# Attention and a gated feed-forward layer: byte-wise dependencies in the list scheduler, and v's and the weights' statistics taken several at a time

## The chip, the core and the metric

The kernel runs on one core of one Trainium2 chip. The metric is the device time of one execution in microseconds. Six names stand for the core's parts below: PE (TensorE, matmuls), PEld (the loading of a matmul's stationary operand), DVE (VectorE), ACT (ScalarE), POOL (GpSimd) and SP (SyncE, which issues transfers here). The engines run side by side, each strictly through its own list of instructions, and meet at semaphores.

## The reference

Eight batches, twelve heads, 448 positions, 64 channels per head. q and k are normalised (root mean square over the channels, times a gain), then attention:

```python
q_n, k_n = (rmsnorm(q, g_q), rmsnorm(k, g_k))
scores = scale * np.matmul(q_n, k_n.transpose(0, 1, 3, 2))
attn = np.exp(scores - np.max(scores, axis=-1, keepdims=True))
attn = attn / (np.sum(attn, axis=-1, keepdims=True) + 1e-09)
x = np.matmul(attn, v)                   # heads side by side: 768 channels
```

The result x goes, per batch, into a feed-forward layer that mixes each position with the one before it:

```python
xk = mu_k * x + (1.0 - mu_k) * x_prev
xr = mu_r * x + (1.0 - mu_r) * x_prev
k = np.maximum(xk @ w_k, 0.0)            # 768 -> 1024
v = k * k @ w_v                          # 1024 -> 768
r = 1.0 / (1.0 + np.exp(-(xr @ w_r)))    # 768 -> 768
out = r * v
```

The three weight matrices come in 64-bit numbers.

## The kernel before

**Numbers.** Most products are made from two float16 halves, a high part and the remainder: three matmuls (high by high, high by low, low by high) stand for one. To split a number well, it is first scaled by a power of two that is taken from a statistic of its tile.

**Attention.** Two heads are a *pair* (48 in all, six per batch), two pairs a *quad*. For each quad k and q are loaded, normalised and turned so that channels lie on partitions (tile `stk`). Seven groups of scores per quad follow (`sc`, five banks of PSUM): DVE finds the largest of each row, ACT takes the exponential and its sum (tile `sums`), DVE makes the reciprocals, and the probabilities are written, turned, to `pT`. Then a pair's product of `pT` with v (called av) is made into a PSUM bank called `ot`. There is one such bank. In batch 0 (quads 0 to 2, pairs 0 to 5, the constant `U32`) all this is done in float32; later pairs use the halves `vh` and `vl` of v.

**v's statistics** (`vprep`). For each pair ACT squares v and sums each partition's squares to one column, `vs`. PE spreads that column over all partitions, with a matmul against the identity into bank `ot`: the column is its stationary operand, read as the upper half of a float32, that is as bfloat16. DVE takes the maximum, makes a power of two `sv` from its exponent in two steps and the inverse `iv` in a third (in `bstat`, six columns of each per batch); then ACT writes `vh` and DVE `vl`. Two buffers `vf` take v as it is loaded, and in batch 0 av reads `vf` itself.

**The weights** (`weights`, `wsplit`). Twenty tiles (8 of w_k, 6 of w_r, 6 of w_v) are turned from 64-bit to float32 (`wf`), and each gets its scale: a matmul of the tile with itself, DVE takes the diagonal (`dg`), a matmul with ones spreads it, DVE takes the maximum and makes the scale in `WSC` and the inverse in `WIN`, one column per tile. Then the tile is split into `wkh`/`wkl`, `wrh`/`wrl` or `wvh`/`wvl`. For the first tiles the buffers `raw` and `wf` are partly borrowed from the later tile `kk`. The inverses are first used when the eight tiles of w_k are done (`RSC`) and when all twenty are (`wdone == NW`).

**The feed-forward layer** (`mixk`, `mixr`, `moe`). As soon as all six pairs of a batch are attended, xk is mixed, and PE makes the products with w_k (into bank `mm`, of which there are two), then with w_r and w_v. The products of batch b are interleaved with the attention of the next.

**What sets the order.** Nothing above is written in the order in which it runs. Each part is a generator that yields its operations, and the class `Plan` is a list scheduler: it keeps a clock for each engine and prices for the operations, and always emits the yielded operation whose start, less a bonus for its priority, is earliest. A start is the later of the engine's clock and the moment at which the operation's operands are free, plus a margin on PE (1200 ns for the matmul of vs). To know the latter, the scheduler records for each operation which tiles it reads and writes, each as a range of elements along the free dimension: `span` (line 142) makes the ranges, `ready` (line 226) compares them. What is emitted stands in the engine's list for good; the semaphores that keep the program right are set by the layer below, whatever the scheduler believes. All operations are recorded at one line, so the profile shows L265 for nearly everything (L272 in the changed kernel) and parts are told apart by tile names.

The lines around `vs`, for a later pair:

```python
yield A.activation(out=vh.bitcast(BF16), in_=vf, func=AF.Square, accum_out=vs[:, 0:1])
pt = yield from banks["ot"].get()
yield T.matmul(form=("v", 60), out=pt[:, 0:P], lhsT=vs[:, 0:1].bitcast(BF16)[:, 1:2]..., rhs=ident16, ...)
```

Of the kernel before, what the change touches and what calls it, by code (L numbers as in the profile page):

```python
# [10 lines left out]
I32 = mybir.dt.int32  # L11
AF = mybir.ActivationFunctionType
# [64 lines left out]
U32 = 3  # L77
SWITCH = 600
# [122 lines left out]
class Plan:  # L201
# [9 lines left out]
    def margin(self, form):  # L211
        if form == "moe":
            return 0
        if form == "av" and self.st["want"] != "xk":
            return MARGIN_A
        return MARGIN_V if form == "v" else MARGIN

# [196 lines left out]
def attn_moe_kernel(tc, q, k, v, g_q, g_k, mu_k, mu_r, w_k, w_v, w_r, out):  # L414
# [41 lines left out]
    LD, SS, VF, VV, TQ, PT, BS, BSC, XT, XK, XKN, XR, CNT, OS, CARRY = {}, {}, {}, {}, {}, {}, {}, {}, {}, {}, {}, {}, {}, {}, {}  # L456
# [6 lines left out]
    def until(f):  # L463
        while not f():
            yield f
# [56 lines left out]
    ring_sum = [small.tile([P, 6], F32, name="sums%d" % n, bufs=1) for n in range(6)]  # L522
# [129 lines left out]
    def turn(w, X, n, u):  # L652
        for a0 in range(0, NT, 4):
# [15 lines left out]
            if u < U32:  # L669
                dst = whole(X[:, n])[:, a0:a0 + m, :]  # L670
                if plan.clk["ACT"] < plan.clk["DVE"]:
# [27 lines left out]

    def vpreps():  # L700
        for i in range(NPAIR):
            st["vi"] = i
            yield from until(lambda: i in VF and st["tq"] >= GATE_V)
            if i < 2 * U32:
                yield from vprep(i, VF.pop(i), None, None)
                continue
            vh = yield from R["vh"].get()
            vl = yield from R["vl"].get()
            yield from vprep(i, VF.pop(i), vh, vl)

    def vprep(i, vf, vh, vl):
        b, hp = pairs[i]
# [3 lines left out]
        vs = small.tile([P, 2], F32, name="vs", bufs=4)  # L716
        if vh is None:
            pt = yield from banks["ot"].get()
            yield A.activation(out=pt.rearrange("p (a c) -> p a c", c=HD), in_=vf, func=AF.Square, accum_out=vs[:, 0:1])
        else:  # L720
            yield A.activation(out=vh.bitcast(BF16), in_=vf, func=AF.Square, accum_out=vs[:, 0:1])
            pt = yield from banks["ot"].get()
        yield T.matmul(form=("v", 60), out=pt[:, 0:P], lhsT=vs[:, 0:1].bitcast(BF16)[:, 1:2].broadcast_to([P, P]), rhs=ident16, start=True, stop=True)
        yield V.tensor_reduce(out=vs[:, 1:2], in_=pt[:, 0:P], axis=AX.X, op=ALU.max)
        banks["ot"].put(pt)
        sv, iv = s_[:, hp:hp + 1], s_[:, NP + hp:NP + hp + 1]
        yield V.tensor_scalar(out=sv.bitcast(I32), in0=vs[:, 1:2].bitcast(I32), scalar1=24, scalar2=23, op0=ALU.logical_shift_right, op1=ALU.logical_shift_left)
        yield V.tensor_scalar(out=sv.bitcast(I32), in0=sv.bitcast(I32), scalar1=-1.0, scalar2=float(204 << 23), op0=ALU.mult, op1=ALU.add)
        yield V.tensor_scalar(out=iv.bitcast(I32), in0=sv.bitcast(I32), scalar1=-1.0, scalar2=float(0x7F000000), op0=ALU.mult, op1=ALU.add)
        if vh is None:  # L730
            VV[i] = vf, None, None
        else:
# [4 lines left out]
        if hp == NP - 1:  # L737
            yield from batch_scales(b)
# [52 lines left out]
    def expo(gi, j, both, sums, D, tp):  # L791
        sp = both[j]
        if tp is not None:
            yield V.tensor_reduce(out=sums[:, j:j + 1], in_=sp[:, 0:S], axis=AX.X, op=ALU.max, negate=True)
            yield A.activation(out=tp.bitcast(F32).rearrange("p a c -> p (a c)")[:, j * S:(j + 1) * S], in_=sp[:, 0:S], func=AF.Exp, bias=sums[:, j:j + 1], accum_out=sums[:, 4 + j:5 + j])
# [7 lines left out]
    def probs(gi, both, sums, D, tp):  # L803
# [15 lines left out]
        r = sums[:, 2:4]  # L819
# [16 lines left out]
    def probs_pe(u, x, t0, sums, tp):  # L836
        r = sums[:, 2:4]
        yield V.tensor_scalar(out=r, in0=sums[:, 4:6], scalar1=1e-9, scalar2=2.0 ** -15, op0=ALU.add, op1=ALU.mult)
# [6 lines left out]
        for a0 in range(0, NT, 4):  # L845
# [6 lines left out]
            if u < U32:  # L852
                dst = whole(PTQ[:, :, :])[:, a0:a0 + m, c0:c0 + P]
                yield A.copy(out=dst, in_=src) if plan.clk["ACT"] < plan.clk["DVE"] else V.tensor_copy(out=dst, in_=src)
# [17 lines left out]
    def attends():  # L872
        for i in range(NPAIR):
# [17 lines left out]
            if vl is None:  # L891
                VFREE.append(vh)
# [92 lines left out]

    def wsplit(nm, kt, c, ci, f):
# [6 lines left out]
        sc, inv = WSC[:, ci:ci + 1], WIN[:, ci:ci + 1]  # L993
# [8 lines left out]
        yield V.tensor_scalar(out=inv.bitcast(I32), in0=sci, scalar1=-1.0, scalar2=float(0x7F000000), op0=ALU.mult, op1=ALU.add)  # L1002
# [164 lines left out]
```

## Time and profile before

| | us |
|---|---|
| median of 3 runs | 1048.58 |
| their range | 1046.12 to 1053.55 |
| the profiled execution | 1048.6 |
| its span, first to last instruction | 1046.8 |
| PE busy | 937.4 (90%) |
| DVE busy | 796.4 (76%) |
| ACT busy | 747.2 (71%) |
| POOL busy | 686.5 (66%) |

A row of a group gives the engine, the operation, output<-input by the program's names, the shapes and the number of instructions, then busy time in us and the mean of one in ns, then the idle time in front of them and what ended it. A row of a wait gives who waited for whom, with the sum in us, the number of times and the longest. A row in order of time gives start, length, engine and operation; in brackets the idle time in front of it and what ended that. PEclk, and the column of the same name in a table of stretches, is the clock that PE was granted as a share of full speed.

### The profile page before, as it was taken

The page shows a single profiled execution, that of the slowest core. Times are in us where ns is not written, and L with a number is a line of the kernel's source. Part 1 is how long each engine was busy: PE and PEld are TensorE (multiplying, and loading weights), DVE is VectorE, ACT ScalarE, POOL GpSimd, SP SyncE. Part 2 cuts the span into 40 slices and gives each one's busy share as a digit, 9 for nine tenths or more (in the row PEclk, how much of TensorE's full clock was granted, in tenths as well). Part 3 has the DMA queues.
Part 4 walks back from the last instruction along what each step waited for, and adds up shares of the span by engine and source line. Part 5 has one row for each costly group of instructions (what it writes and reads, how often), then busy time and mean ns, then how long its engine had stood idle before and what let it go on. Part 6 is the DMA issues. An engine that isn't in the chain of part 4 may idle for free. (4 is left out here: it accounts for less than half of the span.)

```text
span 1046.8 us, 18947 instructions
## 1 busy us (share of the span) xinstructions
PE 937.4 (90%) x6166; PEld 491.6 (47%) x6166; DVE 796.4 (76%) x2001; ACT 747.2 (71%) x1753; POOL 686.5 (66%) x738
## 2 busy tenths in 40 slices
PE   1678685788999999999999999999899999999997
PEld 0344332444554555455545555454345544555564
DVE  4888868997988688968987888879876887884100
ACT  2576748896879688788887778868786888874311
POOL 2587767862778565985796569857595569725811
PEclk9788876999999999999999999999799999999999
DMA  7443347884988799898986898688785897684011
GB/s 200 117 112 105 88 115 161 179 177 95 171 166 153 149 174 172 156 165 160 182 166 117 166 184 170 130 163 168 153 154 120 167 184 155 118 146 84 1 31 31
DMA packets 447043, 146.62 MB, mean 140 GB/s; under 512 B 418784, under 2 KB 443360, under 8 KB 446944
## 3 DMA queue, kind: packets, MB, share of 16 engines
q1 hardware_dynamic: 427408, 127.42, 64.1%
q10 hardware_dynamic: 19536, 18.00, 6.0%
q8 instruction: 48, 0.79, 0.3%
q14 instruction: 51, 0.42, 0.1%
HBM read 50.40 MB, written 11.01 MB: 59 GB/s over the span
## 5 line engine op out<-in xcount | busy, mean ns | idle before, releaser
L265 PE MATMUL mm<-wvh,kk 128*128 128x384 f16 x896 | 233.9, 326 | 0.0
L265 PE MATMUL mm<-xk,wkh 128*128 128x448 f16 x768 | 212.5, 359 | 7.5 <-DVE WSC L265 6.7
L265 DVE TENSOR_REDUCE sums<-sc 128x1 f32<-128x448 f32 x336 | 194.4, 615 | 31.8 <-PE sc L265 31.2
L265 ACT ACTIVATE sc<-sc,sums 128x448 f32<-128x448 f32 x294 | 181.3, 618 | 43.8 <-DVE sums L265 40.4
L265 PE MATMUL mm<-wrh,xr 128*128 128x384 f16 x672 | 178.2, 329 | 0.0
L265 ACT ACTIVATE nat<-sc,sums 128x448 f16<-128x448 f32 (+1 forms) x258 | 157.3, 650 | 26.4 <-DVE sums L265 18.8
L265 PEld LDWEIGHTS <-kk 128*128 128x128 f16 (+1 forms) x1362 | 129.8, 98 | 96.1 <-issue 12.9
L265 DVE SCALAR_TENSOR_TENSOR nat<-sc,sums,nat 128x448 f16<-128x448 f32 x228 | 148.7, 675 | 21.9 <-ACT nat L265 21.7
L265 PE MATMUL mm<-wvl,kk 128*128 128x384 f16 x448 | 146.0, 326 | 0.0
L265 PE MATMUL sc<-stk 64*128 64x448 f16 (+3 forms) x1104 | 132.8, 386 | 11.7 <-DVE nat L265 7.5
L265 PE MATMUL mm<-xk,wkl 128*128 128x448 f16 x384 | 137.4, 358 | 0.0
L265 PEld LDWEIGHTS <-xr 128*128 128x128 f16 x1008 | 96.2, 98 | 74.0 <-issue 14.3
L265 PEld LDWEIGHTS <-wkh 128*128 128x128 f16 x768 | 73.0, 99 | 82.9 <-issue 23.6
L265 PE MATMUL mm<-wrl,xr 128*128 128x384 f16 x336 | 110.3, 328 | 0.0
L265 PE MATMUL ot<-pT,vh 128*64 128x448 f16 x672 | 101.9, 360 | 4.8 <-DMA pT<-natx 2.0
L265 POOL TENSOR_TENSOR o<-o,bsc 128x384 f32<-128x384 f32 x48 | 42.7, 890 | 88.5 <-DVE o L265 55.7
L265 POOL TENSOR_TENSOR qk<-qk,ss 128x896 f32<-128x896 f32 x36 | 63.8, 1773 | 34.2 <-DVE ss L265 31.0
L265 ACT ACTIVATE o<-mm,bsc 128x128 f32<-128x128 f32 x144 | 45.3, 382 | 56.6 <-PE mm L265 44.2
L265 POOL TENSOR_TENSOR nat<-nat 128x448 f32<-128x448 f32 x46 | 54.0, 1175 | 39.0 <-ACT nat L265 38.7
L265 POOL TENSOR_TENSOR nat<-qk,nat 128x896 f16<-128x896 f32 x30 | 57.3, 1911 | 28.2 <-ACT nat L265 28.1
L265 DVE SCALAR_TENSOR_TENSOR o<-o,mm 128x384 f32<-128x384 f32 x56 | 30.6, 547 | 58.1 <-PE mm L265 57.9
L265 DVE SCALAR_TENSOR_TENSOR df<-x,bsc,df 128x448 f32<-128x448 f32 x68 | 64.8, 962 | 10.6 <-POOL df L265 10.5
(167 smaller groups left out, 1799.5 us busy)
## 6 DMA issues: line engine op xcount, KB each, us to landing
out_dram<-o SPq DMA_DIRECT2D x56, 192.0 KB, 3.1
qk<-in_k_dram SPq DMA_DIRECT2D x46, 224.0 KB, 3.8
qk<-in_q_dram SPq DMA_DIRECT2D x108, 64.0 KB, 2.6
vf<-in_v_dram SPq DMA_DIRECT2D x96, 64.0 KB, 2.7
raw<-in_moe_w_v_dram ACTq DMA_DIRECT2D x12, 512.0 KB, 4.8
vf<-in_v_dram SPq DMA_DIRECT2D x96, 48.0 KB, 2.4
raw<-in_moe_w_r_dram ACTq DMA_DIRECT2D x12, 384.0 KB, 3.3
kk<-in_moe_w_k_dram ACTq DMA_DIRECT2D x8, 384.0 KB, 3.9
```

Of the source, the lines that this page charges most:

```text
L265: r = op.fn(op.kw["out"], op.kw["value"]) if op.fn.__name__ == "memset" else op.fn(**op.kw)
```

## The change

Six edits:

- `span` gives ranges in bytes instead of elements (except for `pT`, whose ranges stay as they were). Two views of one tile with different element sizes are now compared rightly.
- In batch 0 `vprep` takes two pairs at a time: each is squared by itself, then two matmuls, one reduction over both, and each of the two steps on two columns. The inverses of the batch's six pairs are made in one step behind the last pair. The later pairs go one by one as before.
- In batch 0 a pair's v is handed to attention (`VV`) before its statistics; its buffer is given back when both the square and av are done (`vfree`).
- The inverses of the weights' scales are made for eight tiles at once, when w_k is done, and for the other twelve when all are.
- In `sums` the row sums and their reciprocals stand in every second column (4 and 6, 8 and 10) instead of side by side; the tile has 12 columns.
- `pick` replaces a comparison of two clocks by the same comparison.

```diff
@@ span
     if t.name.startswith("pT"):
         lo %= 2 * S
         hi = lo + x.ap[-1][1]
+    else:
+        lo, hi = lo * SIZE[x.dtype], hi * SIZE[x.dtype]
...
@@ vpreps, vprep
-        for i in range(NPAIR):
+        i = 0
+        while i < NPAIR:
             st["vi"] = i
...
+            n = V_SIDE if i < 2 * U32 else 1
+            yield from vprep([i + e for e in range(n)])
+            i += n
...
+        vs = small.tile([P, 4], F32, name="vs", bufs=4)
+        vh = vl = pt = None
+        for e, i in enumerate(js):
+            yield from until(lambda: i in VF and st["tq"] >= GATE_V)
+            vf = VF.pop(i)
+            if half:
+                vh = yield from R["vh"].get()
+                vl = yield from R["vl"].get()
+                sq = vh.bitcast(BF16)
+            else:
+                VV[i] = vf, None, None
+                pt = pt or (yield from banks["ot"].get())
+                sq = pt.rearrange("p (a c) -> p a c", c=HD)
+            yield A.activation(out=sq, in_=vf, func=AF.Square, accum_out=vs[:, e:e + 1])
+            if not half:
+                vfree(i, vf)
+                if e < n - 1:
+                    banks["ot"].put(pt)
+                    pt = None
+        pt = pt or (yield from banks["ot"].get())
+        yield [T.matmul(form=("v", 60 * n), out=pt[:, e * P:(e + 1) * P], lhsT=vs[:, e:e + 1].bitcast(BF16)[:, 1:2].broadcast_to([P, P]), rhs=ident16, start=True, stop=True) for e in range(n)]
+        yield V.tensor_reduce(out=vs[:, 2:2 + n], in_=pt[:, 0:n * P].rearrange("p (a c) -> p a c", c=P), axis=AX.X, op=ALU.max)
         banks["ot"].put(pt)
+        sv, iv = s_[:, hp:hp + n], s_[:, NP + hp:NP + hp + n]
...
-        yield V.tensor_scalar(out=iv.bitcast(I32), in0=sv.bitcast(I32), scalar1=-1.0, scalar2=float(0x7F000000), op0=ALU.mult, op1=ALU.add)
...
-        if hp == NP - 1:
+        if hp + n == NP:
+            if not half:
+                yield inverse(s_[:, NP:2 * NP], s_[:, 0:NP])
             yield from batch_scales(b)
...
@@ expo, probs, probs_pe
-    accum_out=sums[:, 4 + j:5 + j])
+    accum_out=sums[:, 4 + 2 * j:5 + 2 * j])
...
-        r = sums[:, 2:4]
+        r = sums[:, 8:11:2]
...
@@ wsplit
-        yield V.tensor_scalar(out=inv.bitcast(I32), in0=sci, scalar1=-1.0, scalar2=float(0x7F000000), op0=ALU.mult, op1=ALU.add)
...
         if ci < NF and st["wkeys"] == NF:
             yield from until(lambda: st["mus"])
+            yield inverse(WIN[:, 0:NF], WSC[:, 0:NF])
...
         if st["wdone"] == NW:
             yield from until(lambda: st.get("rsc"))
+            yield inverse(WIN[:, NF:NW], WSC[:, NF:NW])
```

Since the scheduler decides the order, the edits move instructions throughout. Three places follow; rows of the kernel before carry L265, rows of the changed one L272.

The first is PE's list at v's statistics of pair 10 (of 0 to 47), where the first products with w_r (`wrh`, `wrl`) begin. `stk` are the turned q and k, `xr` the mixed input. Before:

```order
L265 LDWEIGHTS stk_1874
L265 MATMUL sc_2482<-stk_1874 128x448
L265 LDWEIGHTS vs
L265 MATMUL ot_2526<-ident_75,vs 128x128
L265 LDWEIGHTS xr_1746
L265 MATMUL mm_2535<-wrh,xr_1746 128x384
```

and now:

```order
L272 LDWEIGHTS stk_2223
L272 MATMUL sc_2451<-stk_2223 128x448
L272 LDWEIGHTS vs
L272 MATMUL ot_2476<-ident_75,vs 128x128
L272 LDWEIGHTS stk_2223
L272 MATMUL sc_2481<-stk_2223 128x448
```

The matmul of vs stands at the same row of PE's list. Before, the first product follows it; now a group of scores stands between. By the numbers that the build gives to instructions in the order of their placing, the square of this pair on ACT was placed directly ahead of this matmul before (no other matmul between them), and 18 matmuls ahead of it now.

The second place is PE's list at pair 36, between the last products of one batch with w_v (`kk` by `wvh`, `wvl`) and the first of the next with w_k. Before:

```order
L265 LDWEIGHTS stk_8665
L265 MATMUL sc_9127<-stk_8665 128x448
L265 LDWEIGHTS vs
L265 MATMUL ot_9173<-ident_75,vs 128x128
L265 LDWEIGHTS stk_8665
L265 MATMUL sc_9167<-stk_8665 128x448
```

and now:

```order
L272 LDWEIGHTS kk_7838
L272 MATMUL mm_9086<-wvl,kk_7838 128x384
L272 LDWEIGHTS kk_7838
L272 MATMUL mm_9086<-wvh,kk_7838 128x384
L272 LDWEIGHTS vs
L272 MATMUL ot_9120<-ident_75,vs 128x128
```

Before, scores stand in front of the matmul of vs, with none placed between the square and it; now products with w_v do, and 12 of them were placed between.

The third place is DVE's list where the last weight tile is split (`wvl`). Before:

```order
L265 TENSOR_SCALAR WSC<-WSC 128x1
L265 TENSOR_SCALAR bstat<-vs 128x1
L265 TENSOR_SCALAR WIN<-WSC 128x1
L265 TENSOR_SCALAR bstat<-bstat 128x1
L265 SCALAR_TENSOR_TENSOR nat_2363<-sc_2295,sums_108,nat_2363 128x448
L265 TENSOR_SCALAR bstat<-bstat 128x1
L265 TENSOR_SCALAR sst<-sst 128x14
L265 TENSOR_SCALAR sst<-sst,gm 128x14
L265 TENSOR_REDUCE sums_109<-sc_2408 128x1
L265 SCALAR_TENSOR_TENSOR wvl<-wf_2231,WSC,wvh 128x8x128
```

and now:

```order
L272 TENSOR_REDUCE sums_110<-sc_2451 128x1
L272 SCALAR_TENSOR_TENSOR wvl<-wf_2291,WSC,wvh 128x8x128
L272 TENSOR_REDUCE sums_110<-sc_2452 128x1
L272 TENSOR_SCALAR WIN<-WSC 128x12
L272 SCALAR_TENSOR_TENSOR nat_2449<-sc_2366,sums_109,nat_2449 128x448
L272 TENSOR_SCALAR WIN<-WIN,smu 128x6
```

The inverse of one tile stood ahead of the split; now the inverses of twelve tiles stand behind it, ahead of the steps that use them. Up to this split DVE's list holds 28 instructions fewer than before (510 instead of 538), among them two reductions of scores more (71 instead of 69).

More of the change, by code (lines that the diff above doesn't have):

```diff
@@ L11 @@
 I32 = mybir.dt.int32
+SIZE = {F32: 4, I32: 4, F16: 2, BF16: 2, mybir.dt.uint8: 1}
 AF = mybir.ActivationFunctionType
@@ L77 @@
 U32 = 3
+V_SIDE = 2
 SWITCH = 600
@@ L216, in margin, with pick @@
         return MARGIN_V if form == "v" else MARGIN
+    def pick(self, a, b):
+        return a if self.clk[a] < self.clk[b] else b
     def now(self):
@@ L521, in attn_moe_kernel @@
             HOME[name, o] = vw
-    ring_sum = [small.tile([P, 6], F32, name="sums%d" % n, bufs=1) for n in range(6)]
+    ring_sum = [small.tile([P, 12], F32, name="sums%d" % n, bufs=1) for n in range(6)]
     def setup():
@@ L670, in turn @@
                 dst = whole(X[:, n])[:, a0:a0 + m, :]
-                if plan.clk["ACT"] < plan.clk["DVE"]:
+                if plan.pick("ACT", "DVE") == "ACT":
                     yield A.activation(out=dst, in_=src, func=AF.Copy, scale=gc[:, 0:1]) if n == 0 else A.copy(out=dst, in_=src)
@@ L698, in vload, with vfree, vprep @@
             VF[i] = vf
+    def vfree(i, vf):
+        FR[i] = FR.get(i, 0) + 1
+        if FR[i] == 2:
+            VFREE.append(vf)
     def vpreps():
-        for i in range(NPAIR):
+        i = 0
+        while i < NPAIR:
             st["vi"] = i
[L703 to L712, printed above, removed]
+            n = V_SIDE if i < 2 * U32 else 1
+            yield from vprep([i + e for e in range(n)])
+            i += n
+    def vprep(js):
+        b, hp = pairs[js[0]]
+        n, half = len(js), js[0] >= 2 * U32
         if hp == 0:
@@ L715, in vprep @@
         s_ = BS[b]
[L716 to L723, printed above, removed]
@@ L724, in vprep @@
-        yield V.tensor_reduce(out=vs[:, 1:2], in_=pt[:, 0:P], axis=AX.X, op=ALU.max)
+        vs = small.tile([P, 4], F32, name="vs", bufs=4)
[17 more added lines that the diff above has]
+                    pt = None
@@ L728, in vprep @@
+        yield V.tensor_scalar(out=sv.bitcast(I32), in0=vs[:, 2:2 + n].bitcast(I32), scalar1=24, scalar2=23, op0=ALU.logical_shift_right, op1=ALU.logical_shift_left)
         yield V.tensor_scalar(out=sv.bitcast(I32), in0=sv.bitcast(I32), scalar1=-1.0, scalar2=float(204 << 23), op0=ALU.mult, op1=ALU.add)
-        yield V.tensor_scalar(out=iv.bitcast(I32), in0=sv.bitcast(I32), scalar1=-1.0, scalar2=float(0x7F000000), op0=ALU.mult, op1=ALU.add)
-        if vh is None:
-            VV[i] = vf, None, None
-        else:
+        if half:
+            yield inverse(iv, sv)
@@ L794, in expo @@
             yield V.tensor_reduce(out=sums[:, j:j + 1], in_=sp[:, 0:S], axis=AX.X, op=ALU.max, negate=True)
-            yield A.activation(out=tp.bitcast(F32).rearrange("p a c -> p (a c)")[:, j * S:(j + 1) * S], in_=sp[:, 0:S], func=AF.Exp, bias=sums[:, j:j + 1], accum_out=sums[:, 4 + j:5 + j])
+            yield A.activation(out=tp.bitcast(F32).rearrange("p a c -> p (a c)")[:, j * S:(j + 1) * S], in_=sp[:, 0:S], func=AF.Exp, bias=sums[:, j:j + 1], accum_out=sums[:, 4 + 2 * j:5 + 2 * j])
             banks["sc"].put(sp)
@@ L836, in probs_pe @@
     def probs_pe(u, x, t0, sums, tp):
-        r = sums[:, 2:4]
-        yield V.tensor_scalar(out=r, in0=sums[:, 4:6], scalar1=1e-9, scalar2=2.0 ** -15, op0=ALU.add, op1=ALU.mult)
+        r = sums[:, 8:11:2]
+        yield V.tensor_scalar(out=r, in0=sums[:, 4:7:2], scalar1=1e-9, scalar2=2.0 ** -15, op0=ALU.add, op1=ALU.mult)
         yield V.reciprocal(out=r, in_=r)
@@ L853, in probs_pe @@
                 dst = whole(PTQ[:, :, :])[:, a0:a0 + m, c0:c0 + P]
-                yield A.copy(out=dst, in_=src) if plan.clk["ACT"] < plan.clk["DVE"] else V.tensor_copy(out=dst, in_=src)
+                yield A.copy(out=dst, in_=src) if plan.pick("ACT", "DVE") == "ACT" else V.tensor_copy(out=dst, in_=src)
             else:
@@ L891, in attends @@
             if vl is None:
-                VFREE.append(vh)
+                vfree(i, vh)
             else:
@@ L984, in weights, with inverse @@
             plan.spawn(wsplit(nm, kt, c, ci, f), wprio)
+    def inverse(o, i):
+        return V.tensor_scalar(out=o.bitcast(I32), in0=i.bitcast(I32), scalar1=-1.0, scalar2=float(0x7F000000), op0=ALU.mult, op1=ALU.add)
     def wsplit(nm, kt, c, ci, f):
@@ L992, in wsplit @@
         yield [T.matmul(form=("w", 110 * kt), out=pg[:, 0:P], lhsT=w16[:, i, :], rhs=w16[:, i, :], start=(i == 0), stop=(i == kt - 1)) for i in range(kt)]
-        sc, inv = WSC[:, ci:ci + 1], WIN[:, ci:ci + 1]
+        sc = WSC[:, ci:ci + 1]
         sci = sc.bitcast(I32)
```

4 lines of the change are left out of this document (1 added, 3 removed).

## The prediction

> **What bounds the kernel now.** I read the page's first part, then a table of four stretches, then PE's list of waits, then the order of time around the longest of them.
>
> ```profile
> span 1046.8 us, 18947 instructions
> PE 937.4 (90%) x6166; PEld 491.6 (47%) x6166; DVE 796.4 (76%) x2001; ACT 747.2 (71%) x1753; POOL 686.5 (66%) x738
> PEclk9788876999999999999999999999799999999999
> ```
> ```profile
> 0.00:240.78 240.78, 159.73 (x926) 84.53 (x927) 195.05 (x554) 159.13 (x354) 160.55 (x201) 0.86 0.57 137
> 240.78:957.20 716.42, 693.70 (x4749) 359.09 (x4750) 586.29 (x1428) 567.01 (x1350) 489.80 (x497) 0.99 0.83 156
> 957.20:1040.90 83.70, 83.70 (x494) 48.02 (x492) 14.46 (x18) 21.04 (x49) 35.35 (x39) 1.00 0.08 19
> ```
>
> The columns are length, then busy time of PE, PEld, DVE, ACT and POOL, granted clock, DMA share, GB/s. There are three kernels in one. Up to 240.78 us PE is idle for 81 us and DVE is the busiest engine (195 of 241 us): attention of batch 0 and the splitting of 20 weight tiles share DVE. From 240.78 to 957.2 PE is busy for 693.7 of 716.4 us: here the bound is PE, and 22.7 us of idle time is all there is to win besides a lower clock. From 957.2 PE runs products alone without a gap. So an edit counts if it shortens the start, or if it fills PE's idle time in the middle.
>
> All of PE's waits from 240.7 to 957 us, and the longest in order of time:
>
> ```profile
> PE ot L265 <- ACT vh L265: 16.6, 12, 4.6
> PE sc L265 <- DVE nat L265: 5.2, 6, 2.1
> PE ot L265 <- DMA pT<-natx: 2.0, 2, 1.1
> PE ot L265 <- DMA pT<-nat: 1.8, 2, 0.9
> PE ot L265 <- DVE stm L265: 0.7, 1, 0.7
> PE sc L265 <- DMA stk<-nat: 0.7, 1, 0.7
> ```
> ```profile
> 235.40 0.74 PE L265 MATMUL sc<-stk 64*128 64x448 f16 x6
> 240.78 0.23 PE L265 MATMUL ot<-ident,vs 128*128 128x128 bf16 x1 [4.64 <-ACT vh L265]
> 242.87 0.85 PE L265 MATMUL mm<-wrh,xr 128*128 128x384 f16 x2
> 244.79 0.50 PE L265 MATMUL mm<-wrh,xr 128*128 128x384 f16 x2
> ...
> 739.94 0.74 PE L265 MATMUL sc<-stk 64*128 64x448 f16 x6
> 743.84 0.29 PE L265 MATMUL ot<-ident,vs 128*128 128x128 bf16 x1 [3.15 <-ACT vh L265]
> 744.06 1.30 PE L265 MATMUL sc<-stk 64*128 64x448 f16 x6
> 749.88 0.77 PE L265 MATMUL sc<-stk 64*128 64x448 f16 x6
> ```
>
> The largest wait by far, 16.6 us in 12 times, is one small matmul: the one that spreads v's sum of squares (vs) over the partitions, standing in PE's queue in front of ready products until ACT has squared v. And such a wait costs more than itself: six score matmuls take 0.74 us at 739.94, 1.30 us right behind the wait of 3.15 us, and 0.77 us again at 749.88.
>
> **The change part by part.** *Bytes.* vs is written as float32 column 0 and read by PE as bfloat16 element 1. Counted in elements these are [0,1) and [1,2), which don't meet, so the scheduler took the matmul as ready at once; in bytes they are [0,4) and [2,4). The build numbers instructions in the order in which the scheduler placed them. Counted by those numbers, in 14 of the 42 later pairs no other matmul was placed between the square on ACT and its matmul on PE, all 14 among the last 38, which are those from 240.78 on. Now it is one pair, one more has 6 matmuls between, and the other 40 have 12 or more. What do 12 matmuls cover?
>
> ```profile
> 240.85 0.33 PE L265 MATMUL mm<-wrh,xr 128*128 128x384 f16 x1
> 241.01 0.33 PE L265 MATMUL mm<-wrl,xr 128*128 128x384 f16 x1
> 241.18 0.62 PE L265 MATMUL mm<-wrh,xr 128*128 128x384 f16 x2
> ...
> 743.06 0.63 ACT L265 ACTIVATE vh<-vf 128x512 bf16<-128x512 f32 x1
> 743.58 0.20 ACT L265 ACTIVATION_READ_ACCUMULATOR vh<-vf 128x1 f32 x1
> ```
>
> Products start 0.165 us apart (240.85, 241.01, 241.18), so 12 are 2.0 us; the square with its read-out takes 0.7 us (743.06 to 743.78). Two microseconds swallow every wait but the two quoted, of which 4.64 - 2.0 = 2.6 and 3.15 - 2.0 = 1.15 us may stay. The other ten waits mean (16.6 - 7.8) / 10 = 0.9 us; two pairs still placed close keep 1.8 us. So 16.6 - 2.6 - 1.15 - 1.8 = **11.0 us** go. Bounds: 16.6 (all) and 0 (ACT simply runs late against the plan). The number of these matmuls, 48, stays. After them PE finds other work: in the list above no wait of a product (mm) in this stretch shows at all, so what is late next is the matmul of scores on DVE (5.2 us).
>
> *The clock.* Behind the wait that ends at 240.78 two products take 0.85 us (row 242.87), two at 244.79 take 0.50; counted from 241.18, where the slow ones begin, that is 3.6 us at about half pace, 1.8 us lost. From 743.84 to 749.88 it is 6.0 us at half pace, 3.0 lost. I take the first whole and half of the second, since the stretch before 739 had other waits: **3.3 us**; bounds 0 and 4.8. The Trainium skill, page "TensorE: Matmul & The Clock Gate", Part 1, has the clock halved after a whole idle window of about 3.4 us; by it a wait of 3.15 us would cost no clock, and the sum would hold 1.8 us instead of 3.3. The trace differs: the rows at 739.94 and 744.06 show half pace behind 3.15 us, and the measurement decides.
>
> *DVE's small steps.*
>
> ```profile
> L265 DVE TENSOR_SCALAR bstat<-bstat 128x1 int32<-128x1 int32 x96 | 14.2, 147 | 1.5
> L265 DVE TENSOR_REDUCE vs<-ot 128x1 f32<-128x128 f32 x48 | 13.6, 283 | 16.0 <-PE ot L265 16.0
> L265 DVE TENSOR_SCALAR WIN<-WSC 128x1 int32<-128x1 int32 x20 | 2.9, 145 | 0.2
> L265 DVE TENSOR_SCALAR bsc<-WIN,bsc 128x6 f32<-128x6 f32 x16 | 10.2, 660 | 0.0
> L265 DVE TENSOR_SCALAR sums<-sums 128x2 f32<-128x2 f32 x21 | 7.5, 377 | 1.1 <-ACT nat L265 0.8 <-ACT xk L265 0.3
> L265 DVE TENSOR_REDUCE sums<-sc 128x1 f32<-128x448 f32 x336 | 194.4, 615 | 31.8 <-PE sc L265 31.2
> ...
> L265 DVE TENSOR_SCALAR bsc<-WIN,bsc x16: 221/514/1672, 239.1 to 960.1; 128x6 f32<-128x6 f32 x16
> L265 DVE TENSOR_SCALAR sums<-sums x21: 148/163/1635, 39.0 to 136.4; 128x2 f32<-128x2 f32 x21
> ```
>
> (The last two rows give min/median/max in ns.) In batch 0 go 18 one-column steps of 0.147 us and 6 reductions of 0.283; for the weights 20 inversions of 0.145: 2.65 + 1.7 + 2.9 = 7.25 us in 44 instructions. In their place come 3 reductions of 256 columns, between 0.283 and 0.615, on the line between them 0.42; 6 steps of two columns, nearest row sums<-sums; and 3 steps of 6, 8 and 12 columns, nearest row bsc<-WIN. At these rows' means that is 1.25 + 6 x 0.377 + 3 x 0.66 = 5.5 us, so 1.8 us less; at their minima 1.25 + 6 x 0.148 + 3 x 0.221 = 2.8, so 4.5 less; at their maxima 1.25 + 9.8 + 5.0 = 16.1, so 8.8 us more. I take the means: one-column steps hardly vary, steps of two or more do, and the new ones are such.
>
> *Sums in every second column.* The 21 steps sums<-sums would take 21 x 0.15 = 3.2 us at their minimum, and took 7.5; the columns' distance gains between 0 and 4.3 us. No row has such a stride; I take half, 2.2. The Trainium skill, "Vector Engine (DVE) Microarchitecture Reference", section 5.1, speaks against it: a one-source step from SBUF to SBUF enters the two-port mode by its element count, and the stride is no condition; "SBUF — State Buffer", "SBUF: two separate sides", says that in this mode DVE and GpSimd shut each other out. By these the gain is 0 and the term below halves.
>
> DVE's sum is 1.8 + 2.2 = 4.0 us, all before 241 us. DVE is busy for 81% there and the weights' chain, which ends with wvl, passes through it:
>
> ```profile
> PE mm L265 <- DVE WSC L265: 9.6, 5, 2.9
> PE mm L265 <- DVE wf L265: 8.1, 4, 3.3
> ...
> L265 DVE SCALAR_TENSOR_TENSOR wvl<-wf,WSC,wvh x6: 1274/1279/2703, 178.0 to 233.9; 128x1024 f16<-128x1024 f32 x6
> ```
>
> I put half on the path: **2.0 us**, with 8.8 both ways as bounds. The start's order moves too: ahead of the last low half of w_v DVE has 71 reductions of scores instead of 69, one group of scores more. At 69 reductions in 234 us a group is 6.8 us of the start's pace; whether the start ends that much later or attention is that much further on, the products still owed pay it back, so I put 0 and keep 6.8 each way.
>
> *At nothing:* reading one byte in four (the weights' exponents) and the borrowed wf tile are now seen by the scheduler at their true places, which moves a few early steps that lie under PE's 81 us of idle time. v's tiles are handed on before their statistics; attention of batch 0 waits for its probabilities anyway. A matmul of vs moved behind 12 others holds back the reduction, v's scaling and its av by 2 us; v's pairs come every 716/38 = 19 us, so there is room.
>
> **Sum.** The profiled execution took 1048.6 us, its span of 1046.8 and 1.8 around it, and so stands at the median of the runs (1048.58). 1048.6 - 11.0 - 3.3 - 2.0 = 1032.3.
>
> **Rivals.** *The wait comes back at the batch's end (22%).* All vs matmuls and all av products go through the one bank called ot. Holding it 2.0 us longer delays av, x and the mixed xk on which the next batch's products wait. At the seven ends that is 14 us given back of 16.3: 1046. For it: one stretch holds no product at all, from the last of one batch to the first of the next,
>
> ```profile
> 726.74 0.33 PE L265 MATMUL mm<-wvh,kk 128*128 128x384 f16 x1
> ...
> 745.29 0.93 PE L265 MATMUL mm<-xk,wkh 128*128 128x448 f16 x2
> ```
>
> while PE waited for DVE, a transfer and vs in turn. Against it: behind the start the clock falls in one of the page's slices alone, this one, and the list of waits has none of a product.
>
> *A starved end (12%).* The same place, once a late xk leaves PE without any product:
>
> ```profile
> 700.00:725.00 25.00, 24.62 (x176) 12.78 (x175) 22.72 (x52) 19.43 (x48) 17.68 (x16) 1.00 0.81 152
> 725.00:750.00 25.00, 18.60 (x112) 8.03 (x112) 21.92 (x58) 20.09 (x51) 14.24 (x18) 0.73 0.93 178
> ```
>
> There PE did 112 matmuls against 176, 64 x 25/176 = 9 us lost in one end of seven. If PE, no longer held up, reaches four more ends ahead of attention, 36 us go against the 16.3 gained: 1068. It decides from the point where xk's last part comes later than the last product of the batch before; DVE at 22 of 25 us there has little left to hurry with.
>
> *The change does not do it (6%).* ACT is late against the plan whatever is placed between; waits stay and only DVE's 2 us are won: 1047.
>
> **Chances and range.** The forecast holds 60%. What a measurement of this kernel can tell is about 1% (10.5 us; the three runs lie 7 us apart). Below 1038.1: nearly all of the forecast and a little of the first rival, 62%. Within 1%: 25%. Slower: 13%. The range runs from 1020 (16.6 + 4.8 + some 7 of the start's bounds) to 1050, over the forecast with the start's 6.8 against it and the two rivals near 1046; the starved ends stay out.
>
> **What would show it.** PE's waits of ot on ACT vh under 6 us in place of 16.6, none above 3 us; PE idle between the start's end and the last batch near 12 us instead of 22.7, with a granted clock of 1.00 in all slices there. The start's end (first product with wrh) at 234 to 241 us. sums<-sums at 0.15 to 0.2 us mean if the stride helps; bstat on two columns near 0.38. It is wrong if those waits reappear under another name (sc on DVE, mm on xk), or if the start ends past 248 us.

## The result, and the profile after

| | before | after |
|---|---|---|
| median, runs of one job | 1051.07 us (1046.12 to 1054.05) | 1023.3 us (1022.31 to 1024.57) |
| ratio | | 0.9741, 95% interval 0.9695 to 0.9787 |
| span of the profiled execution | 1046.8 us | 1022.8 us |
| first product with w_r (end of the start) | 240.85 us | 235.89 us |
| from there to PE's last matmul | 800.28 us | 781.20 us |
| of it PE idle | 22.7 us | 8.4 us |

The change makes the kernel 2.6% faster; the forecast was 1032 us. First the page of the kernel after: the span, the busy time of each engine, the granted clock in 40 slices.

```profile
span 1022.8 us, 18968 instructions
...
PE 933.2 (91%) x6166; PEld 489.2 (48%) x6166; DVE 789.3 (77%) x1967; ACT 748.2 (73%) x1755; POOL 691.6 (68%) x738
...
PEclk9779889978999999999999999999999999999999
```

Next the table of stretches, cut at the first product with w_r, of the kernel before and then of the kernel after (length, busy PE, PEld, DVE, ACT, POOL, granted clock, DMA share, GB/s).

```profile
0.00:240.85 240.85, 159.80 (x927) 84.60 (x928) 195.05 (x554) 159.13 (x354) 160.55 (x201) 0.86 0.57 137
240.85:1041.13 800.28, 777.56 (x5240) 407.04 (x5240) 600.75 (x1446) 588.06 (x1399) 525.14 (x536) 0.99 0.75 141
```
```profile
0.00:235.89 235.89, 160.43 (x933) 85.18 (x934) 193.42 (x520) 159.45 (x356) 161.20 (x202) 0.88 0.56 141
235.89:1017.09 781.20, 772.79 (x5235) 403.97 (x5233) 595.34 (x1447) 588.73 (x1399) 529.62 (x535) 0.99 0.69 145
```

The 24 us between the two spans are 5.0 from the start, 14.3 of PE's idle time behind it (800.28 - 777.56 = 22.7, now 781.20 - 772.79 = 8.4) and 4.8 of PE's busy time there; what follows the last matmul is 5.7 us in both. One column that the prediction did not look at moved most: the DMA share behind the start went from 0.75 to 0.69, for the same transfers.

PE's waits behind the start, in the kernel after (who waited for whom: sum, times, longest):

```profile
PE ot L272 <- ACT vh L272: 3.1, 1, 3.1
PE sc L272 <- DVE nat L272: 2.9, 5, 1.4
PE ot L272 <- DMA pT<-natx: 1.0, 1, 1.0
PE ot L272 <- DVE vl L272: 0.7, 1, 0.7
PE ot L272 <- DVE bstat L272: 0.3, 1, 0.3
```

The waits of v's matmul on the square fell from 16.6 us in 12 times to 3.1 in one. (Of the 16.6 us, the longest wait, 4.64 us, ended at 240.78 us, just ahead of the first product with w_r: it is idle time of the start, and 12.0 us belong to the 22.7.) That looks like the forecast come true. But the waits on `nat` and on the transfers into `pT` and `stk` fell too (5.2 to 2.9, and 4.5 to 1.0), which nothing in the prediction explains.

The small steps on DVE in the kernel after (busy us, mean ns):

```profile
L272 DVE TENSOR_SCALAR sums<-sums 128x2 f32<-128x2 f32 x21 | 8.6, 426 | 1.2 <-ACT nat L272 1.1
...
L272 DVE TENSOR_SCALAR WIN<-WSC 128x8 int32<-128x8 int32 x1 | 1.3, 1309 | 0.0
L272 DVE TENSOR_REDUCE vs<-ot 128x2 f32<-128x256 f32 x3 | 1.2, 414 | 0.0
L272 DVE TENSOR_SCALAR bstat<-bstat 128x2 int32<-128x2 int32 x3 | 0.7, 239 | 0.0
L272 DVE TENSOR_SCALAR bstat<-vs 128x2 int32<-128x2 int32 x3 | 0.5, 162 | 0.0
L272 DVE TENSOR_SCALAR bstat<-bstat 128x6 int32<-128x6 int32 x1 | 0.2, 171 | 0.0
L272 DVE TENSOR_SCALAR WIN<-WSC 128x12 int32<-128x12 int32 x1 | 0.2, 162 | 0.0
```

Last, the main DMA queue of the kernel before, and then of the kernel after: packets, MB, and the time of the packets as a share of 16 engines' span.

```profile
q1 hardware_dynamic: 427408, 127.42, 64.1%
```
```profile
q1 hardware_dynamic: 427408, 127.42, 59.2%
```

The same 427408 packets took 0.641 x 1046.8 = 671 us (the mean of the 16 engines) before and 0.592 x 1022.8 = 605 us after, a tenth less. The experiments come back to this row.

### The profile page after: what moved, and what is told of

Its sections match the earlier page's. It is cut to its first block, busy times and chain, and to the rows that moved or that the text cites. A ratio compares the mean times of both kernels' runs of the same rounds, so it can differ in the third digit from the quotient of the medians.

```text
span 1022.8 us, 18968 instructions
## 1 busy us (share of the span) xinstructions
PE 933.2 (91%) x6166; PEld 489.2 (48%) x6166; DVE 789.3 (77%) x1967; ACT 748.2 (73%) x1755; POOL 691.6 (68%) x738
## 3 DMA queue, kind: packets, MB, share of 16 engines
q1 hardware_dynamic: 427408, 127.42, 59.2%
## 4 chain that ended last, share of the span: by engine, by line
PE 54%; DVE 18%; ACT 9%; POOL 7%; issue 6%; DMA 4%; SPq 1%; ACTq 0%; POOLq 0%; DVEq 0%
PE mm L272 37%; PE ot L272 9%; PE sc L272 8%; DVE sums L272 4%; DVE nat L272 3%; POOL xk L272 2%; ACT nat L272 2%; ACT sc L272 2%; DVE sst L272 2%; DVE df L272 2%; DMA pT<-nat 1%; DVE stm L272 1%; POOL nat L272 1%; SPq L272 1%; POOL qk L272 1%
## 5 line engine op out<-in xcount | busy, mean ns | idle before, releaser
L272 PE MATMUL mm<-wvh,kk 128*128 128x384 f16 x896 | 234.4, 327 | 0.0
L272 PE MATMUL mm<-xk,wkh 128*128 128x448 f16 x768 | 209.5, 355 | 5.9 <-ACT kf L272 4.2
L272 DVE TENSOR_REDUCE sums<-sc 128x1 f32<-128x448 f32 x336 | 194.3, 614 | 23.4 <-PE sc L272 23.0
L272 ACT ACTIVATE sc<-sc,sums 128x448 f32<-128x448 f32 x294 | 180.9, 617 | 36.9 <-DVE sums L272 33.1
L272 ACT ACTIVATE nat<-sc,sums 128x448 f16<-128x448 f32 (+1 forms) x274 | 167.2, 653 | 24.9 <-DVE sums L272 13.1
L272 PE MATMUL mm<-wrh,xr 128*128 128x384 f16 x672 | 179.9, 331 | 0.0
L272 DVE SCALAR_TENSOR_TENSOR nat<-sc,sums,nat 128x448 f16<-128x448 f32 x242 | 158.3, 675 | 28.0 <-ACT nat L272 27.5
L272 PEld LDWEIGHTS <-kk 128*128 128x128 f16 (+1 forms) x1362 | 129.2, 98 | 97.2 <-issue 17.0
L272 PE MATMUL sc<-stk 64*128 64x448 f16 (+3 forms) x1104 | 135.0, 386 | 12.8 <-DVE nat L272 4.2
L272 PE MATMUL mm<-wvl,kk 128*128 128x384 f16 x448 | 146.0, 326 | 0.0
L272 PE MATMUL mm<-xk,wkl 128*128 128x448 f16 x384 | 135.8, 354 | 0.0
L272 PEld LDWEIGHTS <-xr 128*128 128x128 f16 x1008 | 96.9, 99 | 75.2 <-issue 16.3
L272 PE MATMUL mm<-wrl,xr 128*128 128x384 f16 x336 | 111.3, 331 | 0.0
L272 PEld LDWEIGHTS <-wkh 128*128 128x128 f16 x768 | 72.2, 98 | 80.5 <-issue 19.8
L272 PE MATMUL ot<-pT,vh 128*64 128x448 f16 x672 | 101.0, 359 | 2.6 <-issue 1.3
L272 POOL TENSOR_TENSOR o<-o,bsc 128x384 f32<-128x384 f32 x48 | 42.9, 894 | 78.6 <-DVE o L272 53.9
L272 POOL TENSOR_TENSOR qk<-qk,ss 128x896 f32<-128x896 f32 x36 | 63.3, 1758 | 43.2 <-DVE ss L272 28.5
L272 DVE SCALAR_TENSOR_TENSOR o<-o,mm 128x384 f32<-128x384 f32 x56 | 30.6, 546 | 78.0 <-PE mm L272 49.9
L272 ACT ACTIVATE o<-mm,bsc 128x128 f32<-128x128 f32 x144 | 45.6, 386 | 45.6 <-PE mm L272 33.6
L272 DVE SCALAR_TENSOR_TENSOR df<-x,bsc,df 128x448 f32<-128x448 f32 x68 | 65.7, 978 | 10.5 <-POOL df L272 10.3
L272 PEld LDWEIGHTS <-stk 64*128 64x128 f16 x1008 | 35.7, 98 | 70.7 <-issue 48.9
L272 POOL TENSOR_TENSOR nat<-nat 128x448 f32<-128x448 f32 x41 | 47.5, 1157 | 29.9 <-ACT nat L272 29.2
```

Of the source, the lines that this page charges most:

```text
L272: r = op.fn(op.kw["out"], op.kw["value"]) if op.fn.__name__ == "memset" else op.fn(**op.kw)
```

## The experiments

Each time is a median with its range. Each ratio is to the kernel before, run in the same job, with its 95% interval; that kernel's median lay between 1047.3 and 1051.1 us from job to job. Waits and idle times come from one profiled execution each.

**Is it v's matmul?** The theory of the prediction: the waits of the matmul of `vs` are the lost time, and ranges in bytes take them away. Its first rival: other waits take their place. Three kernels take those waits away in three ways.

The kernel before with ranges in bytes and nothing else of the change:

```diff
+    else:
+        lo, hi = lo * SIZE[x.dtype], hi * SIZE[x.dtype]
```

> The kernel before with one edit: ranges in bytes, as in the change. Theory A (the matmul of vs stood too early): of 42 later pairs 2 are now placed with no matmul between square and spread, against 14; PE's waits of ot on ACT vh fall from 16.6 us to under 5, and the time falls by 14 to 22 us, to 1027 to 1035. Theory B (the grouped small steps of DVE shorten the start): within 5 us of the kernel before, and the first product with w_r no earlier than 239 us. Theory C (any new order moves the time by as much): anything from 1020 to 1060, with no tie to the waits on vh.

1048.38 us (1046.24 to 1049.52), ratio 0.9999 (0.9979 to 1.0020): nothing. Its waits behind the start:

```profile
PE sc L268 <- DVE nat L268: 6.6, 8, 2.2
PE ot L268 <- DMA pT<-nat: 5.3, 6, 1.4
PE ot L268 <- ACT vh L268: 5.2, 1, 5.2
PE ot L268 <- DVE bstat L268: 1.9, 1, 1.9
```

The edit does what it says: 16.6 us in 12 times became 5.2 in one. But PE's idle time behind the start stayed, 23.2 us against 22.7: PE now waits for transfers into `pT` (1.8 us before) and for `nat`.

The same for the tile `vs` alone:

```diff
+    elif t.name.startswith("vs"):
+        lo, hi = lo * SIZE[x.dtype], hi * SIZE[x.dtype]
```

> The kernel before with ranges in bytes for the tile vs alone; the exponent bytes, the borrowed wf and all else stay in elements. Theory A: as the run with bytes everywhere within 5 us, 1027 to 1035, waits on ACT vh under 5 us. If the other views matter (early weight steps in the start), this run stays slower than that one by 5 us or more and its start ends later.

1043.85 us (1041.74 to 1051.86), ratio 0.9961 (0.9931 to 0.9992). The waits on the square are down to 1.4 us, and PE's idle time went up to 28.1 us; waits on transfers into `pT` and `stk` are 13.3 us. What it gained lies ahead of the first product with w_r, at 236.53 us.

And a wider margin for this matmul in the kernel before, ranges left as they are:

```diff
-MARGIN_V = 1200
+MARGIN_V = 3000
```

> The kernel before, ranges in elements, with the margin of the matmul of vs raised from 1200 to 3000 ns: the scheduler still knows nothing of the square but places the matmul later, with 4 instead of 14 pairs with nothing between. Theory A: waits on ACT vh fall to 4 to 8 us and the time to 1032 to 1042. Theory C: no tie, anything from 1020 to 1060. If the time falls only with a rightly known dependency, it stays at 1045 to 1053.

1052.81 us (1045.88 to 1057.25), ratio 1.0035 (1.0007 to 1.0062); waits on the square 4.3 us, PE idle 27.8. So the theory falls: three times most of these waits went, and each time PE waited at least as long in all, for something else.

**Which part carries the gain?** One part taken out of the kernel after, or put alone into the kernel before.

The kernel after with ranges in elements:

```diff
-    else:
-        lo, hi = lo * SIZE[x.dtype], hi * SIZE[x.dtype]
```

> The changed kernel with ranges in elements again; all else as changed. Theory A: 14 later pairs with nothing between, waits on ACT vh of 12 us or more, time 1040 to 1050. Theory B: 1025 to 1035, since the small steps stay grouped. Theory C: anything from 1020 to 1060.

1026.4 us (1025.68 to 1027.58), ratio 0.9784 (0.9741 to 0.9828), as theory B had it: more than four fifths of the gain without the bytes. Waits on the square are 8.3 us, PE idle 13.5 against 8.4 in the kernel after. On top of the rest the bytes are worth 3 us (1026.4 to 1023.3, in two jobs; the intervals of the two ratios overlap).

The kernel after with batch 0's pairs one by one:

```diff
-V_SIDE = 2
+V_SIDE = 1
```

> The changed kernel with v's statistics of batch 0 taken pair by pair again (bytes, the weights' inverses at once, the batch's inverses at once and the stride stay). Theory B1 (the two pairs at once bring batch 0 forward, its first product with w_k at 155 instead of 176 us, and attention keeps that lead): time 1038 to 1052, first product with w_k after 170 us. Theory B2 (the weights' inverses at once do it): 1020 to 1030. Theory C (any new order moves the time by as much): anything from 1020 to 1060.

1031.78 us (1029.72 to 1032.64), ratio 0.9832 (0.9794 to 0.9871): two pairs at once are worth 8.5 us here. The start ends at 240.86 us as in the kernel before, 5.0 us later than in the kernel after. Neither range came true: the first product with w_k is back at 175.92 us (155.50 in the kernel after), as theory B1 had it, but the time lies between B2's range and B1's.

The kernel before with the weights' inverses made at once:

```diff
-        yield V.tensor_scalar(out=inv.bitcast(I32), in0=sci, scalar1=-1.0, scalar2=float(0x7F000000), op0=ALU.mult, op1=ALU.add)
...
+            yield inverse(WIN[:, 0:NF], WSC[:, 0:NF])
...
+            yield inverse(WIN[:, NF:NW], WSC[:, NF:NW])
```

> The kernel before with one edit: the inverses of the weights' scales made for eight and twelve tiles at once; ranges in elements, pairs one by one, sums side by side. Theory B2: 1022 to 1032. Theory B1: 1042 to 1052. Theory C: anything from 1020 to 1060. In its order the first product with w_r stands behind 48 more matmuls than before, as in the changed kernel without bytes, which took 1026.

1043.13 us (1039.63 to 1045.80), ratio 0.9942 (0.9918 to 0.9966), in the range of theory B1. The first product with w_k comes at 159.64 us here, against 175.91 before; little of this lead reaches the end.

The kernel before with two pairs at a time, the early handing on of v and the wider sums, without bytes and with inverses one by one:

```diff
-        for i in range(NPAIR):
...
+            n = V_SIDE if i < 2 * U32 else 1
+            yield from vprep([i + e for e in range(n)])
...
-    ring_sum = [small.tile([P, 6], F32, name="sums%d" % n, bufs=1) for n in range(6)]
+    ring_sum = [small.tile([P, 12], F32, name="sums%d" % n, bufs=1) for n in range(6)]
```

> The kernel before with v's statistics of batch 0 two pairs at a time (and the stride of sums); ranges in elements, the weights' inverses one by one. Theory B1: 1022 to 1034, first product with w_k before 160 us. Theory B2: 1042 to 1052. Theory C: anything from 1020 to 1060.

1061.3 us (1056.38 to 1062.07), ratio 1.0107 (1.0063 to 1.0151): slower than before, and outside all three ranges. Behind the start its waits are

```profile
PE ot L270 <- ACT vh L270: 19.8, 13, 6.8
PE sc L270 <- DVE nat L270: 10.6, 11, 4.5
```

and PE is idle for 33.2 us. With ranges in elements, 18 of the 42 later pairs had no matmul placed between square and matmul, against 14 before: the scheduler's blindness costs more or less as the rest of the order falls. This kernel and the one without bytes differ in the weights' inverses alone, and by 35 us; that is no price of an inverse but of an order. The parts' values don't add up, and a part tried alone says little of its share in the whole.

**What makes the transfers faster?** Of the kernels so far, those with the wide sums tile had q1 at 58.8 to 59.9%, all others at 62.8 to 64.8%. One more run of the same round, meant to price the stride, takes this edit back in the kernel after: sums in neighbouring columns, a tile of 6 columns. The order of the instructions is the same on every engine.

```diff
-    ring_sum = [small.tile([P, 12], F32, name="sums%d" % n, bufs=1) for n in range(6)]
+    ring_sum = [small.tile([P, 6], F32, name="sums%d" % n, bufs=1) for n in range(6)]
...
-        r = sums[:, 8:11:2]
-        yield V.tensor_scalar(out=r, in0=sums[:, 4:7:2], scalar1=1e-9, scalar2=2.0 ** -15, op0=ALU.add, op1=ALU.mult)
+        r = sums[:, 2:4]
+        yield V.tensor_scalar(out=r, in0=sums[:, 4:6], scalar1=1e-9, scalar2=2.0 ** -15, op0=ALU.add, op1=ALU.mult)
```

> The changed kernel with the columns of sums side by side again, in an order of instructions that is the same on every engine: only the addresses differ. If the stride keeps DVE's two-column steps from POOL's locks, as the prediction gave it half a chance, these 21 steps now mean less than here and the time rises by 1 to 4 us. If it does nothing (the steps mean 0.43 us in the changed kernel against 0.38 before): the time stays within 2 us, 1021 to 1026.

1039.55 us (1036.47 to 1040.63), ratio 0.9907 (0.9876 to 0.9939): 16 us of the gain are gone, and neither expected outcome (1 to 4 us more, or no more than 2 us either way) came true. The small steps are not the reason, they took the same:

```profile
L272 DVE TENSOR_SCALAR sums<-sums 128x2 f32<-128x2 f32 x21 | 8.3, 414 | 1.2 <-ACT nat L272 1.1
```

The waits behind the start, and the queue with two kinds of transposing transfers (issues, median us from issue to landing):

```profile
PE sc L272 <- DVE nat L272: 5.9, 8, 2.0
PE ot L272 <- DMA pT<-nat: 4.7, 7, 1.1
PE ot L272 <- ACT vh L272: 2.9, 1, 2.9
PE sc L272 <- DMA stk<-nat: 2.1, 2, 1.6
```
```profile
q1 hardware_dynamic: 427408, 127.42, 64.5%
...
pT<-nat SPq DMA_TRANSPOSE x121, 4.6
...
stk<-nat SPq DMA_TRANSPOSE x28, 4.2
```

In the kernel after these two rows are

```profile
pT<-nat SPq DMA_TRANSPOSE x121, 4.0
...
stk<-nat SPq DMA_TRANSPOSE x28, 3.5
```

One thing differs between these two kernels beside the columns: a sums tile takes 64 instead of 32 bytes of each partition, and with six of them the large tiles that the build places behind them lie 192 bytes further on. By the addresses that the build gives, `pT` starts at byte 78144 of its partitions in the kernel before, 320 past a multiple of 512 (64 past one of 256), and at 78336 in the kernel after, a multiple of 512; `nat`, `stk`, `qk`, `x` and the products' operands shift with it. The theory of addresses against the theory of the stride:

The kernel with sums side by side, and an unused tile of 192 bytes behind them:

```diff
+    small.tile([P, 48], F32, name="pad", bufs=1)
```

> The kernel after with its sums back in six neighbouring columns, as in the run with the sums side by side (1039.6 us), and an unused tile of 192 bytes a partition behind them, so that every later tile (nat, pT, stk, qk, x, the products' operands) starts at the same address as in the kernel after, a multiple of 512 bytes. Nothing reads or writes the unused tile, and the instructions are the same. Address theory: the steps of DMA queue q1 fall back to about 59% of 16 engines' span (64.5% side by side), the median time to landing of the transposes of nat into pT to about 4.0 us (4.6 side by side), and the time to 1021 to 1027 us. Stride theory (the columns' distance itself makes the small steps cheaper): 1037 to 1041 us, with q1 at 64 to 65%.

1024.73 us (1023.34 to 1025.62), ratio 0.9776 (0.9758 to 0.9793), and

```profile
q1 hardware_dynamic: 427408, 127.42, 59.0%
...
pT<-nat SPq DMA_TRANSPOSE x121, 4.0
```

A tile that nothing touches brings 14.8 of the 16 us back (PE idle 8.8 us, against 23.0 without it). In the traces of these two kernels the 403456 packets of 256 bytes on q1 took 22.5 ns each without the tile and 20.0 with it, which makes 61 of the 66 us by which q1's packets fell. The engines' own work did not change: behind the start DVE, ACT and POOL were busy for the same time within 1.2 us, and PE within 1.3. The stride has no effect of its own that shows: 1024.7 against 1023.3 us, with overlapping intervals, and the 21 steps took 349 ns here, 426 in the kernel after. The median of a step is 164 ns in both; the means hang on a few long ones.

The kernel before with the same line (`pad`, 192 bytes) behind its sums, and nothing else of the change:

> The kernel before with nothing but an unused tile of 192 bytes a partition behind its sums, so that the same tiles start at multiples of 512 bytes; element ranges, inverses one by one, pairs one by one, all as before. Address theory: q1 falls from 64.1% to 59 or 60%, landing of nat to pT from 4.6 to about 4.0 us, and the time to between 1030 and 1042 us; it can be less than the 16 us of the pair of runs on the kernel after, since the waits on v's statistics (16.6 us) stay. Stride theory: 1046 to 1053 us, no change.

1038.94 us (1036.67 to 1042.58), ratio 0.9905 (0.9879 to 0.9931):

```profile
q1 hardware_dynamic: 427408, 127.42, 57.5%
...
pT<-nat SPq DMA_TRANSPOSE x114, 3.8
```
```profile
PE ot L265 <- ACT vh L265: 15.3, 11, 4.7
PE sc L265 <- DVE nat L265: 3.0, 3, 2.1
```

8.6 us from one unused tile. Here the waits on transfers are gone and those on the square stay, where bytes alone did the reverse.

The kernel after with the shifted tiles 128 bytes past a multiple of 512:

```diff
+    small.tile([P, 32], F32, name="pad", bufs=1)
```

> The kernel after with an unused tile of 128 bytes a partition behind the sums, so that every later tile starts 128 bytes past a multiple of 512 instead of at one. It tells which grid counts. If 64 or 128 bytes are enough (the slow runs' tiles start at 320, which is a multiple of 64 but not of 128), the time stays at 1021 to 1027 us with q1 near 59%. If the grid is 256 or 512 bytes, it goes to 1033 to 1043 us with q1 at 63 to 65%. The Trainium skill, DMA: Bandwidth & Descriptors, section on how a descriptor splits into AXI transactions, states a grid of 256 bytes for reads; by it this run is slow.

1035.7 us (1034.86 to 1036.95), ratio 0.9883 (0.9865 to 0.9900), with q1 back at 64%: a grid of 128 bytes is not enough.

```profile
q1 hardware_dynamic: 427408, 127.42, 64.2%
...
pT<-nat SPq DMA_TRANSPOSE x121, 4.6
```

The kernel after with the same tiles 256 bytes past a multiple of 512, and v's tile and those of the raw weights on multiples of 256 too:

```diff
+    const.tile([P, 32], F32, name="pad_v")
...
+    small.tile([P, 32], F32, name="pad", bufs=1)
...
+        if tag == "wf1":
+            pool.tile([P, 56], F32, name="pad_s", bufs=1)
```

> The kernel after with all tiles that transfers write or read placed on multiples of 256 bytes: nat, pT, stk, qk, x and the products' operands now start 256 bytes past a multiple of 512, and v's tile (384 past a multiple of 512 in the kernel after) and the tiles of the raw weights (480 past one) start on the grid as well, by three unused tiles. The instructions and their order are those of the kernel after (1023.3 us). If 256 bytes are the grid: 1017 to 1025 us with q1 at 58 to 60%, the lower end if the loads of v and of the weights gain too (they are 28 of 147 MB, and few of the waits that end last). If the grid is 512 bytes: 1032 to 1042 us with q1 at 63 to 65%, and nothing can be said on v and the weights.

1023.33 us (1021.96 to 1024.01), ratio 0.9746 (0.9715 to 0.9777), PE idle 8.7 us:

```profile
q1 hardware_dynamic: 427408, 127.42, 59.1%
...
pT<-nat SPq DMA_TRANSPOSE x121, 4.0
```

So of the offsets tried, a multiple of 256 bytes (0 or 256 past one of 512) is fast, and 64 or 128 past it is not. Placing v and the raw weights on this grid as well gives nothing that can be measured.

## Why the prediction was right, and where it was not

The time lies in the range, 9 us below the forecast, and each of the three terms that the profile can show was of the right kind and too small: idle time behind the start 14.3 us (forecast 11.0, of which 2.0 were to come off the wait of 4.64 us that lies in the start), busy time there 4.8 (3.3), the start 5.0 (2.0).

But the causes were mostly others, and the good number is in large part luck. With the tiles at their old addresses (sums side by side) the change gains 9.8 us (1039.55 against 1049.39 in its job) where 16.3 were forecast; the other 15 to 16 come from the addresses, which stood nowhere in the prediction. In shares of the time: the addresses alone 0.95% (the kernel before, padded), the rest of the change alone 0.93% (sums side by side), both together 2.2 to 2.6%. That is at least their sum; that they help each other is not clear of the noise.

PE's idle time behind the start in us, with the part that is waits on the square in brackets (without the wait just ahead of the first product with w_r, 4.6 us in both kernels before):

| | ranges in elements | ranges in bytes |
|---|---|---|
| tiles off the grid | before: 22.7 (12.0) | bytes alone: 23.2 (5.2); after, sums side by side: 23.0 (2.9) |
| tiles on the grid | before, padded: 15.1 (10.6); after, without bytes: 13.5 (8.3) | after: 8.4 (3.1); sums side by side, padded: 8.8 (3.1) |

- **Bytes, 11.0 us.** That the waits of v's matmul go held: 16.6 us became 5.2 with this edit alone and 3.1 in the whole. The step that failed is the one behind it: "After them PE finds other work ... so what is late next is the matmul of scores on DVE (5.2 us)". With bytes alone the waits on the square behind the start fell by 6.8 us (12.0 to 5.2), and others rose by as much: those of scores on DVE's `nat` and `natx` from 5.2 to 7.3, those on transfers into `pT` and `stk` from 4.5 to 6.7, the rest from 0.7 to 3.2. With bytes for `vs` alone the transfers took 13.3. So the edit alone is worth nothing; on top of all else, with the tiles on the grid, it took 5.1 us of idle time (13.5 to 8.4) and 3.1 us of the time. That slow transfers are what swallowed the rest is the likely reading, but the kernel before with bytes and the padding and nothing else was not run. The first rival's price (1046 us) is near that of bytes alone (1048), but it had the place wrong: no wait of a product on `xk` shows in that run.
- **The clock, 3.3 us.** The slice at a clock of 0.7 is gone and PE's busy time behind the start fell by 4.8 us, the forecast's upper bound. But it fell as much in the padded kernel before (772.73 us), whose waits on the square stayed at 15.3 us, and with bytes for `vs` alone (772.34 us), whose tiles are off the grid. So the fall is tied to no single edit and is no evidence for the bytes. That a wait is followed by half pace held, as the rows of the kernel after behind its one long wait show (start, length, in brackets the idle time ahead):

```profile
335.72 0.35 PE L272 MATMUL mm<-xk,wkl 128*128 128x448 f16 x1
339.16 0.23 PE L272 MATMUL ot<-ident,vs 128*128 128x128 bf16 x1 [3.08 <-ACT vh L272]
...
340.64 0.85 PE L272 MATMUL mm<-wrh,xr 128*128 128x384 f16 x2
...
343.18 0.49 PE L272 MATMUL mm<-wrh,xr 128*128 128x384 f16 x2
```

  Two products take 0.85 us at 340.64 and 0.49 at 343.18. The Trainium skill, page "TensorE: Matmul & The Clock Gate", Part 1, asks for a whole idle window of about 3.4 us; here 3.08 us were enough. In the kernel before 2.07 us were: twelve matmuls of scores behind such a wait took 1.33 us, and 0.76 where no wait stood ahead. The prediction left this place out as a stretch with other waits.

```profile
398.03 0.76 PE L265 MATMUL sc<-stk 64*64 64x448 f16 x12
...
733.22 1.33 PE L265 MATMUL sc<-stk 64*64 64x448 f16 x12 [2.07 <-DVE nat L265]
```

- **DVE's small steps, 1.8 us.** The reduction over 256 columns took 414 ns (estimate 0.42 us), the two-column steps 239 and 162 ns (377), those over 6, 8 and 12 columns 171, 1309 and 162 (660). Together that is 4.1 us for 5.5 estimated, 3.2 us less than before. DVE's busy time in the start fell by 1.6 us, from 195.05 to 193.42, and the start ended 5.0 us earlier, which "half on the path" does not explain. One pair at a time it ends at 240.86 us again, but what shortens it was not settled: the list of waits there changes throughout, two kernels with one pair at a time end it at 236.5 and 236.6 us (bytes for `vs` alone, the wide margin), and one order of instructions ended it at 240.85 us in one profiled execution and at 247.27 in another (before, without and with the unused tile).
- **Sums in every second column, 2.2 us.** The wrong cause, and the largest miss. As a stride it gains nothing: 426 ns a step against 377 before, 414 and 349 in the two kernels side by side. This agrees with the rule that was set against the term, that of the Trainium skill, "Vector Engine (DVE) Microarchitecture Reference", section 5.1, by which a stride does not keep a step out of the two-port mode. Which mode the steps ran in no run shows. But the edit is worth 15 to 16 us by the width of its tile, which shifts the large tiles behind it. Without this side effect the kernel comes out at 1039.6 us, on the other side of the forecast.
- **The order of the start, at 0.** Within its bounds: the products began 5.0 us earlier, inside the 6.8.
- **The rivals of a starved end and of no effect** did not happen: the granted clock shows 9 in all slices from 256 us on (8 in the one in which the start ends), and the waits went.

## What to carry to other kernels

Before costing a wait as won, ask what the engine would wait for if it were gone, and price the whole list in the place where it stands: waits that end close together can hide one another, and here taking most of one kind away gained nothing. Look at where an edit moves the tiles, not only at what it does: six small tiles widened by 32 bytes a partition shifted the rest of memory, and in the final order of instructions that was more than half of the gain. A number that comes out right does not prove the sum behind it; only the run that took this edit back showed the miss. So when a queue's time changes for the same packets, compare start addresses first, and try an unused tile as padding: here one line was worth 8.6 us in one order of instructions and 15 to 16 in another.

## What the runs showed of the hardware

- The start address of tiles in SBUF sets how long their transfers take. With the large tiles on multiples of 256 bytes the 427408 packets of q1 took 598 to 623 us (seven kernels); 64 or 128 bytes past one 659 to 676 us (seven kernels). With the order of instructions kept the ranges are 598 to 605 and 664 to 671. A transfer from `nat` into `pT` landed in 3.8 to 4.0 instead of 4.5 to 4.6 us (medians). The Trainium skill, page "DMA: Bandwidth & Descriptors", section "How a descriptor splits into AXI transactions", says that a descriptor that starts off a boundary of 256 bytes first fetches from the boundary below it, at the cost of extra beats. The grid found here agrees with it. That the extra beats are the cause was not shown, and neither was which of the shifted tiles counts.
- Executions of one kernel differ with the clock that PE is granted: of 25 of the kernel before in one job, the shortest took 1041.80 us at a mean clock of 0.964, the longest 1056.76 us at 0.947. So a single profile can mislead about the start: that of the padded kernel before ends it at 247.27 instead of 240.85 us, with a granted clock of 0.81 there instead of 0.86 and the same 927 matmuls busy for 168.2 instead of 159.8 us. It is the longest of that kernel's four executions; the others took 2 to 6 us less at mean clocks of 0.958 to 0.963 (0.952 in this one). That the addresses lower the clock is not shown.
